# Two mixture-of-experts layers on one core: where the late steps' ends and rank products stand

## Chip, cores and metric

The kernel runs on one core of a Trainium2 chip. The metric is the device time of one execution in microseconds. The kernel before has a median of 907.2 us in three runs (906.87 to 910.54).

## What is computed

An attention over 4 batches, 8 heads and 576 positions gives 2304 rows of 512 numbers. Two mixture-of-experts layers follow, each with 8 experts of hidden width 1024, each row going to one expert:

```python
def _moe2_ref(x, w_gate, w1, w2) -> np.ndarray:
    N, D = x.shape
    E = w_gate.shape[1]
    logits = x @ w_gate
    expert_idx = np.argmax(logits, axis=1)
    ...
    for e in range(E):
        mask = expert_idx == e
        ...
        h = np.maximum(xe @ w1[e], 0.0)
        ye = h @ w2[e]
        out[mask] = gate_w[mask, None] * ye
    return out.astype(np.float32)
```

The first layer (layer 0) takes normalised rows and embeddings for its routing; its output is the second's (layer 1's) input. All arrays are float32.

## The kernel before

Rows are sorted by expert into tiles of 128. A layer is a row of **steps**, one tile and one expert each: 18 at least (`NT1`), up to 28 (`NS`), since each expert's last tile is partly filled. How many there are is known only on the chip. Steps 18 to 27 stand in nested conditions (`tc.If(nt_ > t)`; the jumps carry the lines of `nest.close()`, L1643 in layer 0, L1723 in layer 1); here steps 18 to 21 run and 22 to 27 are absent. Every engine that comes to step 22 jumps to the else branch of that condition, which waits for what the engine has issued and then raises its semaphores by as much as the absent steps would have raised them; so whatever waits for "the last write of this buffer" with an absent step as its last possible writer waits for that branch. POOL's else branch does so for its DMAs with one instruction, `INC_SWDGE_SEM`.

A step (`step`, L1374) has two products, each in three passes over high and low halves of the operands (`Wh` and `Wl`, the weights' halves; `b` and `x`, the activations'): 24 products of 512 columns into `ph0` and `ph1`, and 24 into `py`, in groups of three. ACT applies the Relu into `hs`, PE transposes it into `pt`, ACT and DVE split it into `b`. Where a step's expert is followed by another, its weights come by DMA into `stg`, and ACT (`split_hi`, L922) and DVE (`split_lo`, L925) split them into the buffer that is free.

`begin` (L1343) copies on POOL the four routing columns of the tile's gathered rows into `xca` and gathers the tile after next. `end` (L1350) scales `py` into `ysb` on ACT. In layer 0 POOL then copies the columns to `xcb` and stores `ysb` in `x2`, from which layer 1 gathers; in layer 1 POOL stores `ysb` in the output by an indirect DMA.

In layer 0 a step also routes the rows that the step before it made, for layer 1: PE transposes `ysb` and makes logits in `pm1` (columns 0 to 7), `route2` turns them on DVE and ACT into a one-hot `oh` and the gate weight in `xcb`; ACT's part is `th`, which reads `pm1`. `rank_pe` (L1334) makes two small products into columns 256 to 263 of the same `pm1`, `rank_ev` (L1338) and `place` evict and convert the ranks on DVE. Steps 2 to 16 rank in their middle the rows of two steps before; steps 16 and later (`late`) rank those of the step before, behind their last product. The columns in `xcb` go to `x2` by a DMA from POOL (L1474), for the last step by one from SP (L1681).

Program order within an engine is the order in which the code is written; each engine waits at the instruction that needs another's result. The program's own waits are by tile: `rank_pe` waits for `th`, though it writes other columns.

Of the kernel before, what the change touches and what calls it, by code (L numbers as in the profile page):

```python
# [409 lines left out]
def tile_kernel(ctx, tc, q, k, v, M_prev, z_prev, beta, emb, tau, w1a, w2a, wg, w1b, w2b, out):  # L410
    nc = tc.nc
    B, H, S, D = q.shape
    E, DM, FF = w1a.shape
    NTOK = B * S
    P = 128
    KD, KF = DM // P, FF // P
    NT1 = NTOK // P
    NE = 3
    NS = NT1 + E - 1 + NE
    XR = DM + 4  # L420
    PE_, ACT_, DVE_, SP_, POOL_ = (mybir.EngineType.PE, mybir.EngineType.Activation, mybir.EngineType.DVE, mybir.EngineType.SP, mybir.EngineType.Pool)
# [5 lines left out]
    x1, x2 = x1a[1:], x2a[1:]  # L427

    def ctile(shape, name, dt=F32):
        return cst.tile(shape, dt, name=name)  # L430
# [9 lines left out]
    xg0 = ctile([P, XR], "xg0")  # L440
# [7 lines left out]
    ctl, ini = ctile([P, 2, 8], "ctl", I32), ctile([P, 2, 8], "ini", I32)  # L448
# [133 lines left out]
    def place_(c0, n):  # L582

        sl = slice(c0, c0 + n)
        ri = rtile([P, 8], "ri", I32)[:, 0:n]
        r2 = rtile([P, 8], "r2", I32)[:, 0:n]
        rk = rtile([P, 8], "rk")[:, 0:n]
        V = nc.vector
        V.tensor_copy(ri, rkb[:, sl])
        yield  # L590
        V.tensor_scalar(out=r2, in0=ri, scalar1=7, scalar2=None, op0=ALU.arith_shift_right)
        yield
        V.tensor_scalar(out=ri, in0=ri, scalar1=127, scalar2=None, op0=ALU.bitwise_and)
        yield
        V.tensor_copy(tq[:, sl], r2)
        yield
        V.tensor_copy(rk, ri)
        yield
        V.tensor_tensor(out=ohp[:, sl], in0=iop.unsqueeze(1).to_broadcast([P, n, P]), in1=rk.unsqueeze(2).to_broadcast([P, n, P]), op=ALU.is_equal)

    def place(c0, n):
        for _ in place_(c0, n):
            pass

    class Route1:
# [32 lines left out]
        def rank_pe(self, ps):  # L638
            n, mm = self.n, nc.tensor.matmul
            self.ps = ps[:, 0:n * E].rearrange("p (n e) -> p n e", e=E)  # L640
            mm(ps[:, 0:n * E], tri, self.o.rearrange("p n e -> p (n e)"), start=True, stop=False)
            mm(self.ps, ones, acc.unsqueeze(1).to_broadcast([P, n, E]), start=False, stop=(n == 1))
            for i in range(n - 1):
                mm(self.ps[:, i + 1:], ones, self.o[:, i:i + 1].to_broadcast([P, n - 1 - i, E]), start=False, stop=(i == n - 2))
# [22 lines left out]
        def rank_ev(self):  # L667
            V = nc.vector
            V.tensor_tensor(out=self.t8, in0=self.o, in1=self.ps, op=ALU.mult)
            yield  # L670
            V.tensor_reduce(out=rkb[:, self.sl], in_=self.t8, axis=AX.X, op=ALU.add)
            yield
# [480 lines left out]
    def rows_of(t):  # L1153

        return xgt[t % 2] if t else xg0

    def gather(L, t):
        rows = src[L] if t >= NE else src[L][0:1 + P * (NT1 - (5, 2)[L])]
        return nc.gpsimd.indirect_dma_start(out=rows_of(t), out_offset=None, in_=rows, in_offset=bass.IndirectOffsetOnAxis(ap=idx[:, L, t:t + 1], axis=0))  # L1159
# [4 lines left out]

    xca = [ctile([P, 4], f"xca{i}") for i in range(2)]
    xcb = ctile([P, 4], "xcb")
    hooks = Hooks()
    tile_attention(tc, q, k, v, M_prev, z_prev, beta, ident, x1[:, 0:DM], xp, hooks)

# [131 lines left out]
    def yT_pe():  # L1301
        for kk in range(KD):
            nc.tensor.transpose(pm0[:, P * kk:P * kk + P], ysb[:, P * kk:P * kk + P], ident)

    def yT_ev(yT):
        nc.scalar.activation(out=yT, in_=pm0, func=AF.Copy)
# [31 lines left out]
    def rank_ev(c, count=True):  # L1338
        nc.vector.scalar_tensor_tensor(out=rs_["rj"], in0=pm1[:, 256:256 + E], scalar=1.0, in1=oh[:, c], op0=ALU.mult, op1=ALU.mult, accum_out=rkb[:, c:c + 1])
        if count:  # L1340
            nc.vector.tensor_tensor(out=acc, in0=acc, in1=oh[:, c], op=ALU.add)

    def begin(L, t):  # L1343

        if t:
            nc.gpsimd.tensor_copy(xca[t % 2], rows_of(t)[:, DM:XR])  # L1346
        if 1 < t < NS - 2:
            gather(L, t + 2)

    def end(L, t):  # L1350
        xc = xca[t % 2] if t else xg0[:, DM:XR]
        nc.scalar.activation(out=ysb, in_=py, func=AF.Copy, scale=xc[:, 0:1])  # L1352
        if L == 0:
            nc.gpsimd.tensor_copy(xcb, xc)
            nc.gpsimd.dma_start(out=x2[P * t:P * t + P, 0:DM], in_=ysb)
        else:
            nc.gpsimd.indirect_dma_start(out=out, out_offset=bass.IndirectOffsetOnAxis(ap=xc[:, 1:2].bitcast(I32), axis=0), in_=ysb, in_offset=None,  # L1357
                                         bounds_check=NTOK - 1, oob_is_err=False)

    def hT(i, b):  # L1360
        for kk in range(4):
            nc.tensor.transpose(pts[i][:, P * kk:P * kk + P], b.hs[i][:, P * kk:P * kk + P], ident)  # L1362
        hilo(pts[i], b.h[i])
# [10 lines left out]
    def step(L, t):  # L1374

        s, b = steps[L, t], bufs
        more = 0 < t < NS - 1
        split2 = t > 2
        rt2 = L == 0
        late = t >= NT1 - 2  # L1380
        x = x0 if t == 0 else b.x
        lx = lambda kk: (*x, P * kk)
        lh = lambda kk: (*b.h[kk // 4], P * (kk % 4))
        begin(L, t)
        s.gemm(0, ph0, lx, 0, 0, 3)
        yield
        s.gemm(0, ph0, lx, 0, 3, 9)
        yield
        s.gemm(0, ph0, lx, 0, 9, 12)
        if split2:  # L1390
            s.splits(0, (0, 1))
        nc.scalar.activation(out=b.hs[0], in_=ph0, func=AF.Relu)
        if split2:
            s.splits(1, (0,))

        ahead = (L, t) != (0, NT1 - 1)
        if ahead and split2:
            s.loads(0, (0, 1))
            s.loads(1, (0,))
        yield  # L1400
        s.gemm(0, ph1, lx, 512, 0, 6)
        hT(0, b)
        if rt2:
            yT_pe()
            yT_ev(b.hs[0])
        yield
        rk = L == 0 and 2 <= t <= NT1 - 2
        if rk:
            rank_pe(t - 2)
            rank_ev(t - 2)  # L1410
        s.gemm(0, ph1, lx, 512, 6, 12)
        last_mm[0] = s.lm[1]
        nc.scalar.activation(out=b.hs[1], in_=ph1, func=AF.Relu)
        yield
        if more:
            xT_pe(rows_of(t + 1))
        if rt2:
            parts_pe(b.hs[0])
            parts_ev(b.hs[0])
        if more:  # L1420
            hilo(psx, b.x)
        if rt2:
            route2_iov()
        s.gemm(1, py, lh, 0, 0, 3)
        if split2:
            s.splits(0, (2,), "h")
        hT(1, b)
        if split2:
            s.splits(0, (2,), "l")
        if more:  # L1430
            next_step(L, t + 1)
        yield
        s.gemm(1, py, lh, 0, 3, 6)
        cs = (1, 2, 3)
        if t == NE:
            s.splits(1, cs)
            cs = ()
        gen = iter(())
        if rt2:
            logits_pe(b.hs[0])  # L1440
        yield
        s.gemm(1, py, lh, 0, 6, 9)
        if rt2:
            gen = route2(t - 1)
        next(gen, None)
        next(gen, None)
        if split2:
            s.splits(0, (3,))
        if split2 and cs:
            s.splits(1, cs)  # L1450
        if t == 2:
            s.flags()
            s.splits(0, range(4))
            s.loads(0, range(4))
        if not ahead:
            e2.append(nc.values_load(ini[0:1, 1, 0:1], engines=[SP_], min_val=0, max_val=E - 1))
            s.loads(0, (0, 1))
            s.loads(1, (0,))
        if split2:
            s.loads(0, (2, 3))  # L1460
            s.loads(1, (1, 2, 3))
        drain(gen)
        if rk and ((t - 1) % 6 == 0 or t == NT1 - 2):
            c0 = (t - 2) // 6 * 6
            place(c0, t - 1 - c0)
        for q_ in range(9, 24, 3):
            yield
            s.gemm(1, py, lh, 0, q_, q_ + 3)
        last_mm[1] = s.lm[1]
        if (L, t) == (1, NT1 - 2):  # L1470

            nc.gpsimd.drain()
        if rt2:
            nc.gpsimd.dma_start(out=x2[P * (t - 1):P * t, DM:XR], in_=xcb)  # L1474
            if late:
                rank_pe(t - 1)
                rank_ev(t - 1)
                place(t - 1, 1)
        if not ahead:

            with tc.If(rg["nt"] <= NT1):
                for c in range(8):
                    for ins in split_chunk(c, rg["wv"]):
                        tc.add_to_no_dep_group("n18", ins)
        end(L, t)

    def abreast(a, b, ns=()):

# [104 lines left out]
    ysb = fp.tile([P, DM], F32, name="ysb")  # L1593
# [35 lines left out]
    for t in range(1, NS):  # L1629
# [11 lines left out]
        else:  # L1641
            drain(step(0, t))
    nest.close()  # L1643


    last_mm.clear()
# [65 lines left out]
    for t in range(1, NS):  # L1712
# [8 lines left out]
        else:  # L1721
            drain(step(1, t))
    nest.close()  # L1723


# [29 lines left out]
```

## Time and profile before

| | |
|---|---|
| median of 3 runs | 907.2 us |
| the profiled execution's own time | 905.06 us |
| its span, first to last instruction | 903.2 us |
| PE busy | 870.2 us, 96% |
| DVE, ACT, POOL busy | 502.1, 483.8, 275.3 us |
| mean granted clock of PE | 0.991 |

The span is what the trace shows; 1.86 us of the execution's own time lie around it. Times below are counted from the span's start. Layer 0's steps end at about 611 us, layer 1's at 895.8 us. A name like PEldq is the sequencer of PE, which handles jumps and waits ahead of the engine. `A <- B` in a wait reads: A waited for B.

### The profile page before, as it was taken

How to read it: one execution, taken by the hardware profiler on the slowest of the kernel's cores; microseconds unless marked ns; L12 is line 12 of the kernel's file. 1: busy time of each engine (PE TensorE's matmuls, PEld its weight loads, DVE VectorE, ACT ScalarE, POOL GpSimd, SP SyncE). 2: the span in 40 equal slices, each digit the busy share in tenths (PEclk: the TensorE clock that was granted, in tenths of full speed). 3: DMA queues.
4: the chain of work that ended last, by engine and by line, in shares of the span. 5: the costliest groups of instructions: out<-in, count | busy, mean ns of one | idle time of the engine just before them, and what ended most of it. 6: DMA issues, size and time to landing. Idle time of an engine off the chain costs nothing. (4 is left out here: it accounts for less than half of the span.)

```text
span 903.2 us, 20913 instructions
## 1 busy us (share of the span) xinstructions
PE 870.2 (96%) x5347; PEld 686.9 (76%) x5347; DVE 502.1 (56%) x1585; ACT 483.8 (54%) x972; POOL 275.3 (30%) x375
## 2 busy tenths in 40 slices
PE   6999999999989999998999999998999999999996
PEld 4777777677667777786888877886868888888885
DVE  4655656565684676379535666643567314463430
ACT  3657666666756735376435554532367435564531
POOL 5557635543633011212122312121231212321221
PEclk9999999999999999999999999998999999999998
DMA  7322352411333155359515317111668514384111
GB/s 130 80 52 82 73 170 78 101 40 41 100 111 113 59 211 175 108 165 314 177 49 164 108 37 235 38 49 40 234 203 297 171 48 139 130 305 135 43 38 39
DMA packets 102438, 110.32 MB, mean 122 GB/s; under 512 B 69882, under 2 KB 69882, under 8 KB 102276
## 3 DMA queue, kind: packets, MB, share of 16 engines
q1 hardware_dynamic: 94244, 85.33, 31.1%
q0 software_dynamic: 8032, 23.22, 7.8%
q8 instruction: 54, 0.88, 0.4%
q14 instruction: 108, 0.88, 0.3%
HBM read 90.32 MB, written 19.25 MB: 121 GB/s over the span
## 5 line engine op out<-in xcount | busy, mean ns | idle before, releaser
L1250 PE MATMUL py<-Wh,b 128*128 (+1 forms) x688 | 240.8, 406 | 2.6 <-DVE b L1194 2.4
L1250 PE MATMUL ph<-Wh,b 128*128 (+1 forms) x672 | 226.7, 398 | 0.5 <-ACTq L1261 0.5
L925 DVE TENSOR_TENSOR Wl<-stg,Wh 128x1024 f32 (+1 forms) x120 | 145.5, 1224 | 79.8 <-ACT Wh L922 74.4
L1250 PEld LDWEIGHTS py<-Wh,b 128*128 128x128 f32 x688 | 129.3, 188 | 32.6 <-issue 5.3
L1250 PEld LDWEIGHTS ph<-Wh,b 128*128 128x128 f32 x672 | 126.1, 188 | 26.7 <-ACTq L1261 0.9
L922 ACT ACTIVATE Wh<-stg 128x1024 f32 (+1 forms) x120 | 125.6, 1057 | 25.8 <-DVEq L1261 5.9
L1250 PE MATMUL py<-Wl,b 128*128 (+1 forms) x344 | 134.8, 392 | 0.0
L1250 PE MATMUL ph<-Wl,b 128*128 (+1 forms) x336 | 131.1, 390 | 2.7 <-DVEq L1261 2.7
L1194 DVE TENSOR_TENSOR b<-pt,b 128x512 fp32r<-128x512 f32 x86 | 59.4, 691 | 104.0 <-ACT b L1193 102.2
L287 ACT ACTIVATE att<-psat 128x512 f32<-128x512 f32 (+1 forms) x144 | 66.7, 463 | 70.6 <-PE psat L285 69.5
L308 PE MATMUL psav<-vb,att 128*128 128x128 f32 (+1 forms) x640 | 96.3, 281 | 2.9 <-ACT att L287 2.8
L308 PEld LDWEIGHTS psav<-vb,att 128*128 128x128 f32 x640 | 81.3, 191 | 17.3 <-ACT att L287 5.9
L1357 POOL DMA_INDIRECT out_dram<-ysb,xca x21 | 27.1, 1292 | 190.5 <-ACTq L1261 122.7
L1193 ACT ACTIVATE b<-pt 128x512 fp32r<-128x512 f32 x86 | 51.5, 598 | 62.9 <-PE pt L1362 61.4
L1250 PEld LDWEIGHTS ph<-Wl,b 128*128 128x128 f32 x336 | 63.2, 188 | 14.9 <-DVEq L1261 3.4
L1250 PEld LDWEIGHTS py<-Wl,b 128*128 128x128 f32 x344 | 64.9, 189 | 9.9
L233 DVE CUSTOM_DVE_ANT_0 a<-pss,wmask 128x128 f32<-128x128 f32 (+3 forms) x128 | 61.0, 485 | 19.2 <-PE pss L255 11.0
L268 ACT ACTIVATE a<-a,mx 128x128 f32<-128x128 f32 (+3 forms) x128 | 71.2, 556 | 0.4 <-DVE mx L233 0.3
L1352 ACT ACTIVATE ysb<-py,xca 128x512 f32<-128x512 f32 x42 | 28.8, 686 | 76.5 <-PE py L1250 65.8
L1159 POOL DMA_INDIRECT xg<-x_scratch,idx x48 | 55.6, 1157 | 38.4 <-issue 14.9
L1474 POOL DMA_DIRECT2D x_scratch<-xcb x21 | 11.9, 566 | 162.1 <-DVE xcb L1332 59.4
L285 PE MATMUL psat<-ident,a 128*128 128x128 f32 x320 | 56.9, 276 | 1.0 <-ACT a L268 0.8
(380 smaller groups left out, 1280.4 us busy)
## 6 DMA issues: line engine op xcount, KB each, us to landing
stg<-in_moe_w_dram SPq DMA_DIRECT2D x120, 512.0 KB
x_scratch<-ysb POOLq DMA_DIRECT2D x22, 256.0 KB
qkn<-in_q_dram SPq DMA_DIRECT2D x32, 128.0 KB
qkn<-in_k_dram SPq DMA_DIRECT2D x32, 128.0 KB
vb<-in_v_dram SPq DMA_DIRECT2D x32, 128.0 KB
x_scratch<-xb SPq DMA_DIRECT2D x16, 256.0 KB
x_scratch<-stg SPq DMA_DIRECT2D x11, 258.0 KB
xg<-x_scratch,idx POOLq DMA_INDIRECT x48
```

Source lines behind the costliest of these rows:

```text
L233: nc.vector.tensor_tensor_reduce(out=out, in0=ps, in1=mask, scale=1.0, scalar=bound, op0=ALU.add, op1=ALU.min, accum_out=m)
L268: nc.scalar.activation(out=a[:, 0:N], in_=a[:, 0:N], func=AF.Exp, scale=-1.0, bias=mx, accum_out=rs_t[pi][:, c, j:j + 1])
L285: nc.tensor.transpose(ps[:, 128 * i:128 * i + 128], x, ident)
L287: nc.scalar.activation(out=att[:, 0:N], in_=ps[:, 0:N], func=AF.Copy)
L308: nc.tensor.matmul(av_t[pi][:, c, j:], att[:, 128 * kb:128 * kb + 128], vn[:, kb, j:, 0:D], start=(kb == 0), stop=(kb == c))
L922: return nc.scalar.activation(out=chunk(Wh, c, wv), in_=stg[:, c].unsqueeze(1), func=AF.Copy).ins
L925: return nc.vector.tensor_tensor(out=chunk(Wl, c, wv), in0=stg[:, c].unsqueeze(1), in1=chunk(Wh, c, wv).bitcast(F32), op=ALU.subtract).ins
L1159: return nc.gpsimd.indirect_dma_start(out=rows_of(t), out_offset=None, in_=rows, in_offset=bass.IndirectOffsetOnAxis(ap=idx[:, L, t:t + 1] ...
L1193: nc.scalar.activation(out=hi, in_=ps, func=AF.Copy)
L1194: nc.vector.tensor_tensor(out=lo, in0=ps, in1=hi.bitcast(F32), op=ALU.subtract)
L1250: mm = nc.tensor.matmul(ps, x[:, col:col + P], W, start=(first and q_ == qs[0]), stop=(last and q_ == qs[-1]))
L1352: nc.scalar.activation(out=ysb, in_=py, func=AF.Copy, scale=xc[:, 0:1])
```

## The change

From step 17 on (`TE`), `end` of a step no longer stands at the step's end: it stands in `begin` of the next step, inside that step's condition, and for the last step that runs behind the whole nest, as `end(0, None)` and `end(1, None)`. The columns of steps 17 and later are copied into one buffer of their own, `xcn`, so that the end behind the nest need not know the step's number. Behind the nest of layer 0 SP, not POOL, stores `ysb`, at a row worked out from the number of steps, which it loads into a register. In steps 16 and later of layer 0 `rank_pe`, `rank_ev` and `place` stand ahead of the last two groups of three products, no longer behind the last.

```diff
--- before.py
+++ after.py
@@ -1164,6 +1164,7 @@
 
     xca = [ctile([P, 4], f"xca{i}") for i in range(2)]
     xcb = ctile([P, 4], "xcb")
+    xcn = ctile([P, 4], "xcn")
     hooks = Hooks()
     tile_attention(tc, q, k, v, M_prev, z_prev, beta, ident, x1[:, 0:DM], xp, hooks)
 
@@ -1340,19 +1341,32 @@
         if count:
             nc.vector.tensor_tensor(out=acc, in0=acc, in1=oh[:, c], op=ALU.add)
 
+
+    TE = NT1 - 1
+
+    def xc_of(t):
+        return xg0[:, DM:XR] if t == 0 else xca[t % 2] if t < TE else xcn
+
     def begin(L, t):
 
+        if t > TE:
+            end(L, t - 1)
         if t:
-            nc.gpsimd.tensor_copy(xca[t % 2], rows_of(t)[:, DM:XR])
+            nc.gpsimd.tensor_copy(xc_of(t), rows_of(t)[:, DM:XR])
         if 1 < t < NS - 2:
             gather(L, t + 2)
 
     def end(L, t):
-        xc = xca[t % 2] if t else xg0[:, DM:XR]
+
+        xc = xcn if t is None else xc_of(t)
         nc.scalar.activation(out=ysb, in_=py, func=AF.Copy, scale=xc[:, 0:1])
         if L == 0:
             nc.gpsimd.tensor_copy(xcb, xc)
-            nc.gpsimd.dma_start(out=x2[P * t:P * t + P, 0:DM], in_=ysb)
+            if t is None:
+                nl = nc.values_load(ini[0:1, 0, 3:4], engines=[SP_], min_val=NT1, max_val=NS)
+                nc.sync.dma_start(out=x2[bass.ds((nl - 1) * P, P), 0:DM], in_=ysb)
+            else:
+                nc.gpsimd.dma_start(out=x2[P * t:P * t + P, 0:DM], in_=ysb)
         else:
             nc.gpsimd.indirect_dma_start(out=out, out_offset=bass.IndirectOffsetOnAxis(ap=xc[:, 1:2].bitcast(I32), axis=0), in_=ysb, in_offset=None,
                                          bounds_check=NTOK - 1, oob_is_err=False)
@@ -1466,23 +1480,24 @@
         for q_ in range(9, 24, 3):
             yield
             s.gemm(1, py, lh, 0, q_, q_ + 3)
+            if late and rt2 and q_ == 15:
+                rank_pe(t - 1)
+                rank_ev(t - 1)
+                place(t - 1, 1)
         last_mm[1] = s.lm[1]
         if (L, t) == (1, NT1 - 2):
 
             nc.gpsimd.drain()
         if rt2:
             nc.gpsimd.dma_start(out=x2[P * (t - 1):P * t, DM:XR], in_=xcb)
-            if late:
-                rank_pe(t - 1)
-                rank_ev(t - 1)
-                place(t - 1, 1)
         if not ahead:
 
             with tc.If(rg["nt"] <= NT1):
                 for c in range(8):
                     for ins in split_chunk(c, rg["wv"]):
                         tc.add_to_no_dep_group("n18", ins)
-        end(L, t)
+        if t < TE:
+            end(L, t)
 
     def abreast(a, b, ns=()):
 
@@ -1641,6 +1656,7 @@
         else:
             drain(step(0, t))
     nest.close()
+    end(0, None)
 
 
     last_mm.clear()
@@ -1721,6 +1737,7 @@
         else:
             drain(step(1, t))
     nest.close()
+    end(1, None)
 
 
 # ---- launch: one core; inputs and outputs as the reference has them ----
```

Three places of the order. The first is PE at the end of a late step of layer 0 (this is step 19; the same piece stands in steps 16 to 27; `pm` is `pm1`, `Activation_49` and `DVE_49` are ACT's and DVE's semaphores). Before:

```order
L1250 MATMUL py<-Wh_4134,b_4237 128x512
L1250 REGISTER_ALU
L1250 MATMUL py<-Wl_4136,b_4237 128x512
L1250 MATMUL py<-Wh_4134,b_4238 128x512
L1335 LDWEIGHTS tri [waits DVE_49]
L1335 MATMUL pm_4141<-oh,tri 128x8 [waits Activation_49]
L1336 LDWEIGHTS ones
L1336 MATMUL pm_4141<-acc,ones 128x8
L1643 COMPARE_AND_BRANCH
L1250 ISA
L1250 MATMUL ph_4147<-Wh_4133,b_4233 128x512
```

Now:

```order
L1251 MATMUL py<-Wh_4135,b_4238 128x512
L1251 REGISTER_ALU
L1251 MATMUL py<-Wl_4137,b_4238 128x512
L1251 MATMUL py<-Wh_4135,b_4239 128x512
L1336 LDWEIGHTS tri [waits DVE_49]
L1336 MATMUL pm_4142<-oh,tri 128x8 [waits Activation_49]
L1337 LDWEIGHTS ones
L1337 MATMUL pm_4142<-acc,ones 128x8
L1251 ISA
L1251 MATMUL py<-Wh_4135,b_4238 128x512
L1251 REGISTER_ALU
L1251 MATMUL py<-Wl_4137,b_4238 128x512
```

The two rank products with their waits for `oh` (DVE) and `th` (ACT) stood behind the step's last product, and stand now with six products behind them.

The second is ACT at the end of layer 0: the last conditional step's `th`, the else branches (the row with x10) and layer 1's first instruction (L1306 or L1307). Before:

```order
L1277 UNCONDITIONAL_BRANCH
L1325 ACTIVATE th<-pm_4141,mn 128x8 [waits DVE_49]
L1352 ACTIVATE ysb<-py,xca_110 128x512 [waits DMASW1_49,PE_49,Pool_49]
L1643 UNCONDITIONAL_BRANCH
L1643 UNCONDITIONAL_BRANCH [waits Activation_49] x10
L1306 ACTIVATE hs_4229<-pm_4146 128x512 [waits PE_49,Activation_49]
```

Now:

```order
L1278 UNCONDITIONAL_BRANCH
L1326 ACTIVATE th<-pm_4142,mn 128x8 [waits DVE_49]
L1658 UNCONDITIONAL_BRANCH
L1658 UNCONDITIONAL_BRANCH [waits Activation_49] x10
L1362 ACTIVATE ysb<-py,xcn 128x512 [waits DMASW3_49,DMASW2_49,DMASW4_49,DMASW1_49,DMASW5_49,DMASW0_49,DMASW6_49,PE_49,DMASW7_49,Activation_49,Pool_49]
L1307 ACTIVATE hs_4230<-pm_4147 128x512 [waits PE_49,Activation_49]
```

`ysb` stood ahead of the jump and waits now behind it, for the counts of all eight POOL DMA semaphores (`DMASW`), which absent steps would have raised too.

The third is POOL at the end of layer 1, the last store of the output. Before:

```order
L1277 UNCONDITIONAL_BRANCH
L1357 DMA out_dram<-ysb,xca_110 2304x512 [waits DMASW5_49,Activation_49]
L1723 UNCONDITIONAL_BRANCH
L1723 ISA [waits Pool_49,DMASW6_49]
L1723 UNCONDITIONAL_BRANCH
```

Now:

```order
L1739 ISA [waits Pool_49,DMASW4_49,DMASW5_49,DMASW3_49,DMASW6_49,DMASW2_49,DMASW7_49,DMASW1_49,DMASW0_49]
L1739 UNCONDITIONAL_BRANCH
L1371 DMA out_dram<-ysb,xcn 2304x512 [waits DMASW4_49,DMASW5_49,DMASW3_49,DMASW7_49,DMASW1_49,Activation_49]
L1766 UNCONDITIONAL_BRANCH
L1766 ISA [waits barrier_Pool_Activation_PE_DVE_SP_gather]
```

The store stood ahead of the else branches (`ISA` is the instruction that raises the DMA semaphores) and stands now between them and the program's end (L1766).

## Rows read from the trace of the kernel before

**Rows 1.** Waits of PE from 285 us to the end: total us, times, longest
```profile
PE py L1250 <- DVE b L1194: 2.4, 2, 1.5
```

**Rows 2.** Line L1643, 609 to 619 us: ns min/median/max, first and last start
```profile
L1643 POOLq EVENT_SEMAPHORE  x5: 17/42/2449, 614.2 to 616.9; - x5
L1643 PEldq COMPARE_BRANCH  x2: 185/1751/3317, 609.3 to 612.8; - x2
L1643 ACTq COMPARE_BRANCH  x2: 38/42/45, 611.2 to 613.8; - x2
L1643 DVEq COMPARE_BRANCH  x2: 47/55/63, 612.2 to 615.4; - x2
L1643 POOLq COMPARE_BRANCH  x2: 38/42/45, 613.7 to 618.6; - x2
L1643 POOLq INC_SWDGE_SEM  x1: 1544/1544/1544, 617.0 to 617.0; - x1
```

**Rows 3.** Timeline at the end of layer 0: start, us, instruction, [idle before <-releaser]
```profile
608.76 0.27 ACT L1325 ACTIVATE th<-pm,mn 128x8 f32<-128x8 f32 x1 [2.00 <-DVE t8s L1320]
611.01 0.56 POOL L1474 DMA_DIRECT2D x_scratch<-xcb  x1 [9.62 <-DVE xcb L1332]
611.23 0.17 DVE L1339 SCALAR_TENSOR_TENSOR rj<-pm,oh 128x8 f32<-128x8 f32 x1 [0.52 <-PE pm L1336]
611.23 0.69 ACT L1352 ACTIVATE ysb<-py,xca 128x512 f32<-128x512 f32 x1 [2.21 <-PE pm L1336]
613.46 0.19 POOL L1354 COPY xcb<-xca 128x4 f32<-128x4 f32 x1 [1.89 <-DMA x_scratch<-xcb]
613.84 0.50 PE L1250 MATMUL ph<-Wh,x 128*128 x1 [2.65 <-ACTq L1643]
615.37 0.80 PE L1250 MATMUL ph<-Wl,x 128*128 x1 [1.04 <-DVEq L1643]
617.97 1.06 PE L1303 MATMUL pm<-ident,ysb 128*128 128x128 f32 x4
```

**Rows 4.** Two stretches: busy us of PE, PEld, DVE, ACT, POOL; granted clock; DMA
```profile
611.20:614.60 3.40, 0.50 (x1) 0.19 (x1) 1.15 (x9) 0.69 (x1) 1.10 (x3) 1.00 0.06 13
614.60:621.50 6.90, 6.13 (x15) 4.18 (x15) 0.23 (x1) 0.60 (x1) 1.13 (x2) 0.51 0.13 44
```

**Rows 5.** Timeline of layer 0's step 19
```profile
580.02 3.25 ACT L922 ACTIVATE Wh<-stg 128x1024 f32 x3 [0.78 <-DVEq L1261]
581.47 0.29 DVE L1323 TENSOR_SCALAR oh<-t8s,km,xcb 128x8 bf16<-128x8 f32 x1
581.88 0.62 PE L1250 MATMUL py<-Wh,b 128*128 x2
583.17 0.25 ACT L1325 ACTIVATE th<-pm,mn 128x8 f32<-128x8 f32 x1
583.47 0.18 PE L1335 MATMUL pm<-oh,tri 128*128 128x8 bf16 x1
```

**Rows 6.** Timeline of layer 0's step 18
```profile
567.99 0.29 DVE L1323 TENSOR_SCALAR oh<-t8s,km,xcb 128x8 bf16<-128x8 f32 x1
569.80 0.18 PE L1335 MATMUL pm<-oh,tri 128*128 128x8 bf16 x1
```

**Rows 7.** Timeline and line L1723 (as group 2) at the end of layer 1
```profile
896.90 1.02 POOL L1357 DMA_INDIRECT out_dram<-ysb,xca  x1 [9.79 <-ACT ysb L1352]
...
L1723 POOLq EVENT_SEMAPHORE  x5: 17/42/43, 900.5 to 900.8; - x5
```

**Rows 8.** Line L1749, the program's end, and DMA rate in 40 slices, 896 to 903.3 us
```profile
L1749 SPq EVENT_SEMAPHORE  x14: 17/28/28, 901.2 to 903.2; - x14
L1749 POOLq DRAIN  x3: 46/109/945, 901.5 to 903.0; - x3
L1749 SPq DRAIN  x3: 7/7/13, 902.0 to 902.7; - x3
...
GB/s 0 0 0 0 45 0 0 135 0 0 45 0 0 224 314 382 314 68 45 45 22 22 0 0 0 0 0 45 0 0 0 0 0 0 0 0 0 0 0 0
```

## Prediction

> **What bounds the kernel now.** PE is busy for 96% of the span, so I read the waits of PE first: from 285 us on there are few. The largest are two in a row at the end of layer 0, 2.65 and 1.04 us, for ACT's and DVE's sequencers [rows 3]; two stalls of 1.2 us on average on DVE's `b` come next [rows 1], in steps that the change does not touch. A step's end costs PE nothing in between: the next step's first product follows the last of `py` directly, and ACT scales `py` beside it. So moving the end inside running steps can gain nothing; only the places without a next step can: the end of layer 0, where layer 1 begins, and the end of layer 1, where nothing follows.
>
> **End of layer 0, now.** The jump over the absent steps is dear. ACT takes it at 611.2, with `ysb`, and has raised its semaphore at 613.8: 2.6 us. DVE takes it at 612.2, under the conversion of the ranks, and is through at 615.4: 3.1 us to its first wait behind it. PE's takes 3.32 us from 609.3, when its sequencer was ahead of the products [rows 2]. Layer 1's first product wants weights whose last possible writer is an absent step of ACT; it starts at 613.84, at ACT's semaphore. The second wants DVE's, and starts at 615.37, with 1.04 us idle [rows 3]. [...]
>
> **The change, part by part.**
>
> *Restart of layer 1: -0.48 us.* ACT's last work ahead of the jump is now `th`, dispatched at 608.76, so its semaphore comes near 608.8 + 2.6 = 611.4, before PE has ended its jump (609.3 + 3.32 = 612.6). ACT is out of it. DVE is not: the second product still waits for DVE's jump. The rank products come 6 x 0.227 = 1.36 us sooner, but `rj` at 611.23 had waited only 0.52 us for them [rows 3]; before that DVE was making `xcb`. So it starts at 610.75, its jump is taken 0.48 us sooner and the second product starts at 615.37 - 0.48 = 614.9. Bounds: a jump as short as ACT's 2.6 us gives -1.0; one as long as POOL's at the end (3.6 us, below) gives 0. I take its own 3.1.
>
> *The new stall in step 19: +1.36 us.* The rank products wait for `th` by the program's order. In step 19 ACT splits three weight chunks first (580.02, 3.25 us), and `th` runs from 583.17 to 583.42. The rank product ran at 583.47, behind the last product [rows 5]; its new place is six products, 583.24 - 581.88 = 1.36 us, earlier, at 582.11. PE gets there with `oh` ready (581.76) and `th` not, and takes instructions in order: it waits until 583.47 and the six products come behind. Nothing on PE later absorbs it [rows 1], so layer 0 ends 1.36 us later. This is the largest loss.
>
> *The other late steps: +0.15 us.* In step 18 `oh` ends at 568.28, and the rank's new place is 569.80 - 1.36 = 568.44 [rows 6]: 0.16 us of margin, less than the weight load of `tri` ahead of the product needs. In step 21 `th` is done at 609.03 [rows 3], some 0.6 us ahead of the rank's new place; steps 16, 17 and 20 have no splits ahead of it. 0 to 0.3 us together, an estimate of up to two such margins.
>
> *The last `ysb` of layer 0: nothing, if it is in time.* It waits now for POOL's else branch. POOL's jump follows the columns' store of 611.01, which has landed by 613.46, where the copy waiting for it starts [rows 3]; the branch waits for that landing (five waits 0.08 us apart, as in [rows 7]) and raises the DMA semaphores, which took 1.54 us [rows 2]: 615.4. ACT, as many waits and the scaling (0.69 us [rows 3]) later, has `ysb` at 616.4; PE wants it five products after the second, which was 2.60 us behind it [rows 3]: 614.9 + 2.6 = 617.5. Cover 1.1 us. SP's new store goes out while SP waits for the routing columns of the same rows, which DVE makes later in layer 1's first step; without that cover it would delay only POOL's later gathers.
>
> POOL's own jump here took 613.7 to 614.2, 0.5 us [rows 2], at the end of layer 1 up to 3.6 (below). [...] With 3.6 us the branch begins at 611.06 + 3.6 = 614.7, and `ysb` is there at about 617.7, 0.2 us late. The sum goes by 0.5.
>
> *End of layer 1: -1.4 us.* Now POOL issues the last store at 896.90 and jumps; its first wait in the else branch stands at 900.5, after which it raises the semaphores and, at 901.5, drains for 0.945 us; SP's last checks run from 901.2 to its own drain at 902.0, and the end is at 903.2 [rows 7, 8]. After the change POOL and ACT have jumped while PE still makes the last step's products (POOL's work in a step is over some 9.8 us before the store), so behind the store there is only the landing, SP's checks (0.8 us), and the barrier (0.8 us), POOL's drain lying beside them. The store's traffic thins from 899.1 and is over by 900.0 (slices of 0.18 us) [rows 8], POOL's wait puts the landing at 900.5 at the latest. End: landing + 1.7 us. With 899.6 it is 901.3 (-1.9), with 900.5 it is 902.2 (-1.0); I take the middle.
>
> *Inside the running steps: nothing.* `ysb` and POOL's copies and stores stand one branch later, about 0.04 us; ACT had 2.21 us idle before `ysb`, POOL 9.6 us before its store [rows 3]. Without that cover it would be 0.04 us in each of four steps.
>
> **Sum.** +1.36 + 0.15 - 0.48 - 1.4 = -0.37 us. On the profiled execution's own 905.06 us that is 904.7. The median of the runs shown lies 2.1 us above that execution; I add the sum to the median: 907.2 - 0.4 = **906.8 us**. By the bounds alone, 1.36 + 0 - 1.0 - 1.9 = -1.5 and 1.36 + 0.3 + 0 - 1.0 = +0.7: 905.7 to 907.9.
>
> **Rivals.**
>
> *The last `ysb` is late (slower).* Mechanism: POOL's jump and its raising of semaphores stand ahead of a transposition on PE that had no such wait. For it: the long waits of POOL [rows 2]. Against it: 1.1 us of cover at the low clock. It decides once `ysb` comes later than PE does, and that is easiest at the full clock, where the five products take about 1.3 us: PE arrives at 616.2, `ysb` in the worst case at 617.8, a wait of 1.6 us. With the small gain at the end: 907.2 + 1.36 + 0.15 - 0.48 + 1.6 - 1.0 = 908.8 us.
>
> *The clock does not fall (faster).* PE's idle time at the restart shrinks from 3.7 to about 3.2 us, in two pieces with a product between. Should the low stretch be missing, its 6.13 busy us [rows 4] would take half: -3.0, so 903.8 us. For it: PE stood still for up to 1.5 us elsewhere [rows 1] in a run whose mean clock is 0.991. Against it: 3.2 us is nearer to the 3.7 that came with the fall.
>
> *The stall of step 19 is not there.* If `th` came by 582.1, 905.4 us. Against it: the three splits stand ahead of it in ACT's order, and nothing of them is moved.
>
> *The end gains nothing.* If SP's checks and the landing cost what POOL's branch did (the jump was hidden behind the landing anyway), 908.2 us. For it: POOL's first wait and the landing lie within 0.5 us of each other.
>
> **How the numbers follow.** My case 0.55, `ysb` late 0.14, no fall of the clock 0.14, no stall in step 19 0.07, nothing at the end 0.10. The range takes in my own bounds and reaches to the first two rivals, with a little for the runs' own spread (3.7 us between three runs): 903.6 to 909.0. A difference of 0.5% is 4.5 us, about what a measurement of this kernel tells from none. No single case goes so far: faster takes the clock and the missing stall together (902.4), slower a late `ysb` with a longer low stretch of the clock. Faster 0.05, same 0.92, slower 0.03.
>
> **What would show it.** Right: in the waits of PE a new one of about 1.4 us of the rank product for `th` in step 19; the wait for ACT's jump gone, that for DVE's longer (1.2 us or more) with the second product about 3.7 us after the last of `py` instead of 4.2; the end 5.5 to 6.5 us after the last product instead of 7.4. Wrong: PE waiting for `ysb` at the transpositions of layer 1's first step; no wait for `th`; a granted clock of 1.00 all through layer 1's first step, or a low stretch much longer than 6.9 us.

## The result and the profile after

The changed kernel takes 915.96 us (median of 6 runs, 912.69 to 920.36); the kernel before, 907.42 (6 runs, 904.22 to 910.54). The ratio is 1.0109, 95% interval 1.0080 to 1.0139: slower by 8.5 us. I had forecast 906.8 and a range of 903.6 to 909.0. The profiled execution took 913.22 us, 8.2 more than the one of before; its page begins:

```profile
span 911.1 us, 20949 instructions
PE 878.5 (96%) x5347; PEld 687.7 (75%) x5347; DVE 500.3 (55%) x1585; ACT 484.1 (53%) x972; POOL 274.7 (30%) x374
```

PE is busy 8.3 us longer (870.2 before) with the same products, at a mean clock that is no lower (0.996 against 0.991). So most of the time is not in waits. The waits of PE in the changed kernel (total us, times, longest), the largest of the steps:

```profile
PE ph L1251 <- ACT ysb L1362: 5.2, 1, 5.2
PE ph L1251 <- DVEq L1262: 2.4, 2, 1.2
PE py L1251 <- DVE b L1195: 1.9, 2, 1.2
PE pm L1336 <- ACT th L1326: 1.1, 1, 1.1
```

The first stands for the two waits of [rows 3] at the restart, 3.7 us together. The last is the new stall of step 19.

**Where the time went.** I took the start of each step's two rows of products in both traces and looked at how the difference grows. It grows in nearly every step of both layers, by about 0.2 us a step, also where the change moves nothing. In the second half of one `py` (timeline of PE, a step of layer 1; the eight `Wl` products of a `py` are every third product, and these are the fifth and the last, 9 products apart), the kernel before:

```profile
757.57 0.39 PE L1250 MATMUL py<-Wl,b 128*128 x1
...
759.61 0.39 PE L1250 MATMUL py<-Wl,b 128*128 x1
```

and the changed kernel in the same step:

```profile
764.14 0.39 PE L1251 MATMUL py<-Wl,b 128*128 x1
...
766.24 0.40 PE L1251 MATMUL py<-Wl,b 128*128 x1
```

2.04 us against 2.10: a product is issued every 227 ns before, every 233 after, with no wait between and both at the granted clock 1.00. Over all products of layer 1's stretch from 640 to 890 us the median is 227 and 234 ns. Between the start of layer 0's first product and that of layer 1's last second product, 9.75 us are lost; some 6.5 of them are this pace, by the run with the tile alone below. Ahead of that stretch the changed kernel's trace is 0.9 us shorter (the one of before has a stretch at the low clock there, 283.5 to 286.9 us, which the other has not), and behind it the end gains 1.2.

The other places, as forecast or not. Step 19 (timeline): `th` has not moved in its step, PE waits 1.14 us for it, and the six products come behind; from the start of that step's second product to the next step's first, the change loses 1.35 us, as worked out (1.36). Some 0.1 of that is the pace; in the change without its tile, below, the same stretch loses 1.36 without it.

```profile
584.69 0.25 ACT L1326 ACTIVATE th<-pm,mn 128x8 f32<-128x8 f32 x1
584.99 0.17 PE L1336 MATMUL pm<-oh,tri 128*128 128x8 bf16 x1 [1.14 <-ACT th L1326]
```

The restart of layer 1. The jump's line, 609 to 621 us (columns as in [rows 2]):

```profile
L1658 ACTq COMPARE_BRANCH  x2: 38/42/45, 611.8 to 614.8; - x2
L1658 PEldq COMPARE_BRANCH  x2: 3071/3204/3338, 612.8 to 616.4; - x2
L1658 DVEq COMPARE_BRANCH  x2: 47/55/63, 615.0 to 618.1; - x2
```

The timeline of the same stretch:

```profile
614.02 0.40 PE L1251 MATMUL py<-Wh,b 128*128 x1
618.83 0.69 ACT L1362 ACTIVATE ysb<-py,xcn 128x512 f32<-128x512 f32 x1 [6.75 <-DMA x_scratch<-xcb]
619.60 0.79 PE L1251 MATMUL ph<-Wh,x 128*128 x1 [5.19 <-ACT ysb L1362]
622.32 0.93 PE L1304 MATMUL pm<-ident,ysb 128*128 128x128 f32 x4
```

Three stretches behind the last `py` product, as in [rows 4]:

```profile
614.40:619.50 5.10, 0.01 (x1) 0.00 (x0) 0.79 (x5) 0.67 (x1) 0.66 (x2) 1.00 0.04 10
619.50:622.30 2.80, 2.70 (x6) 2.04 (x7) 0.23 (x1) 0.02 (x1) 1.79 (x3) 0.51 0.46 120
622.30:626.00 3.70, 3.70 (x24) 2.74 (x23) 0.29 (x1) 1.20 (x2) 0.30 (x1) 0.91 0.47 132
```

Before, PE's second jump took 0.185 us [rows 2]; now it takes 3.07, from 616.4 to 619.4, and the first product starts right behind it. The row names `ysb` as what the product waited for; but in the program that product waits on ACT for the weights' split alone, which ACT's else branch had signalled at 614.7, and `ysb` happens to end at the same time. The changed kernel with 128 bytes, below, bears this out: there the first product starts 0.3 us before `ysb` ends, and the row of its wait names nothing:

```profile
PE ph L1253 <- issue: 5.0, 1, 5.0
```

In all five kernels whose layer 0 ends behind the nest (this one and four below) the product starts 0.16 us behind the end of PE's jump. `ysb` itself is ready 2.8 us ahead of its transposition.

The low clock lasts 3.4 us, not 6.9 [rows 4]: 0.51 up to 622.3, and 0.91 on the mean of the next 3.7 us, since it is back at 1.00 from 623.0. So the restart loses 2.7 us at its first product and has them back by its second row of products: 0.95 since the second product no longer waits (0.58 us behind the first, 1.53 before), the rest, 1.7 by an estimate, since 3.4 us fewer run at a granted clock of 0.51. The short stretch does not follow from the change alone. In the traces of the changed kernel with two tiles and with 128 bytes, which have the long jump too, the clock stays low for 6.8 us, and the restart costs 1.4 and 0.6 us; in the first of the runs with three distances, whose order is that of before, it is low for 3.4.

The end, in the timeline (before: [rows 7, 8]):

```profile
904.34 0.40 PE L1251 MATMUL py<-Wh,b 128*128 x1
905.73 0.69 ACT L1362 ACTIVATE ysb<-py,xcn 128x512 f32<-128x512 f32 x1 [5.21 <-PEq L1739]
906.69 1.01 POOL L1371 DMA_INDIRECT out_dram<-ysb,xcn  x1 [8.75 <-ACT ysb L1362]
```

and in the lines of layer 1's jump and of the program's end:

```profile
L1739 PEldq COMPARE_BRANCH  x2: 187/1799/3411, 902.0 to 905.7; - x2
L1766 SPq EVENT_SEMAPHORE  x13: 17/28/28, 909.4 to 911.0; - x13
```

From the start of the last product to the end it is 6.7 us, 7.9 before. The store comes 0.8 us later behind that product than before, since `ysb` waits for PE's jump (3.41 us): behind the nest, `py`'s last writer may be an absent step.

### The profile page after: what moved, and what is told of

It reads as the page before. It is cut to its first block, busy times and chain, and to the rows that moved or that the text cites. A ratio compares the mean times of both kernels' runs of the same rounds, so it can differ in the third digit from the quotient of the medians.

```text
span 911.1 us, 20949 instructions
## 1 busy us (share of the span) xinstructions
PE 878.5 (96%) x5347; PEld 687.7 (75%) x5347; DVE 500.3 (55%) x1585; ACT 484.1 (53%) x972; POOL 274.7 (30%) x374
## 5 line engine op out<-in xcount | busy, mean ns | idle before, releaser
L1251 PE MATMUL py<-Wh,b 128*128 (+1 forms) x688 | 244.1, 410 | 2.1 <-DVE b L1195 1.9
L1251 PE MATMUL ph<-Wh,b 128*128 (+1 forms) x672 | 230.2, 403 | 0.5 <-ACTq L1262 0.5
L1251 PE MATMUL ph<-Wl,b 128*128 (+1 forms) x336 | 133.5, 397 | 2.4 <-DVEq L1262 2.4
L1371 POOL DMA_INDIRECT out_dram<-ysb,xca x16 | 20.5, 1280 | 148.5 <-ACTq L1262 88.1
L1406 ACT ACTIVATE hs<-ph 128x512 f32<-128x512 f32 x42 | 25.0, 596 | 55.5 <-PE ph L1251 53.1
```

The source lines that it names most:

```text
L1251: mm = nc.tensor.matmul(ps, x[:, col:col + P], W, start=(first and q_ == qs[0]), stop=(last and q_ == qs[-1]))
```

## The experiments

Times are medians, or the time of one execution where it says so; the kernel before was run again beside each group. "Distance" is how far the tiles `b` stand behind the weights' tiles in a partition, modulo 256 bytes: 0 in the kernel before (`Wh0` at byte 69344, `b0` at 217056; the four weights' tiles, and the six `b`, agree modulo 256), 224 in the changed one, where the new tile `xcn` takes 32 bytes ahead of the weights.

**One tile, nothing moved.** Kernel before with

```diff
     xcb = ctile([P, 4], "xcb")
+    ctile([P, 4], "xcn")
```

> The kernel before, with one more tile of four columns behind xcb that nothing uses: the weights' tiles Wh and Wl stand 32 bytes higher in a partition, as in the changed kernel, and no instruction is moved. Placement theory: the 512-column products are issued every 234 ns in the median, not every 227, and the time is 7 to 9 us above before (914 to 916). Rival (the pace belongs to the moved instructions): 227 ns and 907. Rival (it is chance of the runs): no tie to the kernel, 905 to 910.

912.0 us against 905.49, ratio 1.0082 (1.0053 to 1.0111): 6.5 us. The pace is the changed kernel's, 9 products in 2.10 us:

```profile
759.67 0.40 PE L1251 MATMUL py<-Wl,b 128*128 x1
...
761.77 0.39 PE L1251 MATMUL py<-Wl,b 128*128 x1
```

A tile that no instruction touches costs three quarters of the loss. The instructions' order is excluded as the cause of the pace; the spread of the runs too.

**The changed kernel with a second unused tile** (distance 192).

> The changed kernel with a second unused tile, so that the weights' tiles stand 64 bytes higher than in the kernel before. If the place within 64 bytes decides: 227 ns between products, and about what I forecast plus the restart as traced, 907 to 908.5. If any shift costs: 234 ns and 916. If the moved instructions set the pace: 234 ns and 916.

909.84, ratio 1.0057 (1.0033 to 1.0082). Neither: the median is 230 ns in layer 1 and 231 in layer 0. 64 bytes further is better than 32 (234 in the changed kernel) and worse than none (227).

**Activations 32 bytes lower, weights in place** (distance 224), by a tile of four columns behind the `b` tiles.

> The kernel before, with an unused tile on the right side of the memory: the activations' tiles (x, hs, ysb, xg, b) stand 32 bytes lower, the weights where they were. If the weights' own place decides: 227 ns, 907. If the place of weights and activations relative to each other decides: 234 ns and 914 to 916.

913.46, ratio 1.0095 (1.0066 to 1.0124), 234 ns. It is not the weights' own place.

**Both** (distance 192).

> Both unused tiles: weights 32 bytes higher, activations 32 bytes lower, so that both have left their places within 64 bytes. If the weights' own place decides: 234 ns, 914 to 916. If the relative place decides: 227 ns, 907.

907.92, ratio 1.0032 (1.0013 to 1.0051), 229 ns in layer 1 and 231 in layer 0, which is neither of what I had expected. It is as in the second run, whose distance is the same: the distance decides, but not modulo 64.

**The changed kernel with 128 bytes** (xcn and three more tiles, distance 128).

> The changed kernel with three more unused tiles: the weights' tiles stand 128 bytes higher than in the kernel before, 96 higher than in the changed one. If the distance between weights and activations, taken modulo 128 bytes, sets the pace: 227 ns between products as in the kernel before, and what is left is the change's own: stall of step 19 +1.3, restart of layer 1 about 0 (a second jump of PE of 3 us against a shorter stretch at the low clock), end -1.2; 0 to +2 us against before, with the clock's low stretches as the difference. If only the old distance itself is good: 231 to 234 ns, +5 to +9 us.

914.91, ratio 1.0106 (1.0085 to 1.0126), 232 ns. The period is not 128 bytes. In two kernels further down which have the same distance (the end in layer 1 alone, and both ends) only the places of the moves can be read.

**The ranks alone, no tile.** `rank_pe`, `rank_ev` and `place` ahead of the last two groups, as in the diff.

> The kernel before, with only the ranks moved ahead of the last two groups; no tile is added. Stall theory: PE waits 1.1 us for th in step 19, layer 0 ends 1.3 us later; at the restart DVE's jump comes 0.5 us sooner but ACT's stays: +0.8 to +1.5 us. Rival (something later on PE absorbs the stall): 0.

907.43 against 905.47, ratio 1.0024 (1.0011 to 1.0036): +2.0 us. The late steps lose 1.33 us in the trace, and the stall is there:

```profile
585.36 0.25 ACT L1325 ACTIVATE th<-pm,mn 128x8 f32<-128x8 f32 x1
585.66 0.17 PE L1335 MATMUL pm<-oh,tri 128*128 128x8 bf16 x1 [1.20 <-ACT th L1325]
```

Behind the restart's second product PE stood still for another 1.56 us in this one profile; what held it the trace does not name.

**The end in layer 1 alone** (distance 128), `end` guarded with `L and`.

> The kernel before, with the end moved in layer 1 alone (the ranks and layer 0 stay; the tiles stand 128 bytes higher). With 227 ns between products: -1.2 us, the end 12.5 us after the last step's second product begins, not 13.7. With 231 to 234 ns the pace costs 4 to 9 us on top, and the end's 1.2 us is seen in the trace alone.

911.22, ratio 1.0079 (1.0057 to 1.0101): the pace's price. In the trace, last product to end: 6.92 us against 7.88.

**Both ends, ranks where they were** (distance 128).

> The changed kernel (tiles 128 bytes higher than before) with the ranks back behind the last product. Stall theory: no wait for th in step 19, 1.3 us less than the run with the ranks moved. At the restart DVE's jump comes as late as before, so the second product waits for it (about 4.2 us after the last of py) unless PE's second jump is the long one again (5.2 us).

910.9, ratio 1.0083 (1.0058 to 1.0109). No wait for `th`, and the late steps lose nothing but the pace. PE's second jump is the long one again, 2.95 us.

**The change without its tile.**

```diff
-    xcn = ctile([P, 4], "xcn")
+    xcn = xca[1]
```

> The change with all its moves, but without the new tile: xcn is the second of the two old buffers, xca1, which is free from step 17 on. Every tile stands where it stands in the kernel before. Placement theory: 227 ns between products; the steps drift by no more than 0.02 us each against before, and the time is before plus the moves: stall +1.3, restart -0.6 to +1.4, end -1.2, so -0.5 to +1.5 us; about 7 us less than the changed kernel. Rival (the moved instructions set the pace, and the tiles added theirs in the other runs): 234 ns and +8 us.

907.81 against 906.11, ratio 1.0014 (0.9996 to 1.0032): +1.7 us, where the change with the tile had +8.5. The pace is that of before:

```profile
758.75 0.39 PE L1251 MATMUL py<-Wl,b 128*128 x1
...
760.79 0.39 PE L1251 MATMUL py<-Wl,b 128*128 x1
```

This is the kernel that I had costed. Its trace against that of before: late steps of layer 0 +1.34 us, from there to layer 1's first second product -0.07, the rest of layer 1 +2.10, the end -0.72.

**The end in layer 1 alone, without a tile.**

> The kernel before with the end moved in layer 1 alone and xcn as xca1, no tile added. Placement theory: 227 ns between products, -1.2 us. Rival (the end's gain is inside the spread of the restart and cannot be timed): -0.3 to +0.3 us, with the 1.2 us in the trace.

904.11 against 906.11, ratio 0.9984 (0.9963 to 1.0005). The fastest by its median of the kernels that ran more than once; its interval still touches 1. Its trace shows 0.76 us of the 2.0 at the end: `ysb` waits for PE's jump here too,

```profile
896.33 0.69 ACT L1362 ACTIVATE ysb<-py,xca 128x512 f32<-128x512 f32 x1 [5.59 <-PEq L1738]
```

1.9 us behind the start of the last product, where before it came at 0.6.

**Kernel before, weights 256 bytes higher** (distance 0), and **32 bytes lower** (distance 32, `k1` and `ntl` put into one tile).

> The kernel before with an unused tile of 256 bytes a partition: the weights stand 256 bytes higher. If the distance to the activations counts modulo 256 bytes: 227 ns. If it does not: 229 to 234 ns.

> The kernel before with two small tiles put into one: the weights stand 32 bytes lower. If the pace depends on how far the distance is from the old one, to either side: 234 ns, as for 32 bytes higher. If one side is better than the other: below 227 or near 231 ns.

One execution each: 903.89 us and 227 ns; 911.81 us and 233 ns. 256 bytes more change nothing and 128 do, so the period is 256 bytes as far as these runs show; both sides of 0 are bad.

**Three distances in one program**, twice; the `b` tiles made 2304 bytes long and their content shifted inside:

```diff
-    ... fp.tile([P, 512], F32R, name=f"b{i}") if i < 6 ...
+    off = (4, 24, 40)
+    ... fp.tile([P, 576], F32R, name=f"b{i}")[:, off[i // 2]:off[i // 2] + 512] if i < 6 ...
```

> The kernel before, with the activations' tiles 2304 bytes long instead of 2048 and their content shifted inside: the two that the first product reads by 16 bytes, those of the first half of the second product by 96, those of its second half by 160; the weights stand as before. If a product's own two operands set its pace: three paces in one run, 230 to 236 ns for 96 and 160 (shifts of 32 to 128 gave 231 to 235), and for 16 a value between 227 and 235, or lower than 227 if the old place is not the best. If the pace belongs to the placement of the whole program: one pace in all three.

> As the run with 16, 96 and 160 bytes, with 4, 8 and 192 bytes. If own operands set the pace: 192 like 64 to the other side, about 231 ns; 4 and 8 near 227, or, if the pace falls off with the very first bytes, 230 to 235.

917.14 and 910.56 us beside 904.86, one execution each. The second run has `off = (1, 2, 48)`, which is 4, 8 and 192 bytes. In it the second half of `py` (192 bytes) is faster than the product of the next step that follows it (4 bytes). The first two rows of PE's timeline are six products apart, and so are the last two:

```profile
761.60 0.39 PE L1250 MATMUL py<-Wl,b 128*128 x1
...
762.97 0.39 PE L1250 MATMUL py<-Wl,b 128*128 x1
...
764.35 0.39 PE L1250 MATMUL ph<-Wl,b 128*128 x1
...
765.74 0.40 PE L1250 MATMUL ph<-Wl,b 128*128 x1
```

1.37 us (228 ns each) and 1.39 (232 ns). So the pace goes with the operands of the product itself, not with the program. Mean time from one product's start to the next, layer 1 from 640 to 890 us (pairs with a transposition between them left out; the first half of `py` takes some 231 also at distance 0, and stands apart: 231 at 8 bytes, 234 at 96):

| distance, bytes | ns | runs |
|---|---|---|
| 0 | 226.7 to 226.8 (`ph` 227.5 to 227.7) | before, ranks alone, change without tile, end of layer 1 without tile, 256 |
| 4 | 232.3 (`ph`) | second of the three-place runs |
| 16 | 233.3 (`ph`) | first of them |
| 32 | 233.2 | 32 bytes lower |
| 128 | 232.6 to 232.7 | three kernels with 128 bytes |
| 160 | 233.2 | first of the three-place runs |
| 192 | 228.7 to 228.9 | two tiles, both sides, second of the three-place runs |
| 224 | 233.3 to 233.4 | changed kernel, one tile, right side |

(Without `ph` the value is that of `py`'s second half.)

## Why the prediction was wrong

**The step that failed** is "Inside the running steps: nothing." It costed the two instructions that stand one branch later and not the tile that the same edit adds. `xcn` is allocated ahead of the weights' tiles, moves them by 32 bytes against the activations, and so slows most of the 2112 products: by 4 to 7 ns in `ph` and in the second half of `py`, by 0 to 2 in its first half. That is 6.5 us by the run with the tile alone. By the means it would be some 9, an estimate; a part comes back in waits (those for DVE's `b` shrink from 2.4 us [rows 1] to 1.9). No row of the trace of before shows it, since there all tiles stand at distance 0 (227 ns); what could have been seen ahead of the run is that the tile's line stands in front of the weights' allocation. The forecast, its range and all four rivals took the products' pace as given, so no case could hold the result.

**The moves**, read from the changed kernel and from the change without its tile:

- Stall of step 19, +1.36, and other late steps, +0.15: right. 1.34 together without the tile. Steps 16, 18 and 20 lose 0.32, 0.15 and 0.10 us in that trace and get nearly all of it back in the step behind. In step 18 I had held the load of `tri` to need more than the margin of 0.16 us; it takes 0.10 before and in the changed kernel, but from the end of `oh` to its start it is 0.19 there.
- Restart, -0.48: DVE's jump came as much earlier as worked out (its first wait behind it 4.0 us after the last `py` product began, 4.55 before), and ACT was out of it. But the bound was neither: PE's second jump took 3 us, and I had carried over its 0.185 us, so the second product came 5.8 us after the last of `py`, not 3.7. The jump was 2.8 to 3.1 us long in all five kernels with layer 0's end behind the nest and 0.18 to 0.19 in the eleven others. What makes it long or short no run shows. In the change without its tile the restart comes to -0.07 in sum, and that is in part luck: the low clock lasted 3.4 us in that trace too, and where it lasted 6.8 the same order lost 0.6 and 1.4.
- The last `ysb` of layer 0, nothing: right. It was there 5.5 us after the last `py` product began (5.65 worked out), and 2.8 us ahead of need, more than the cover of 1.1, since PE came late.
- End of layer 1, -1.4 (-1.0 to -1.9): too large. -1.16 in the changed kernel, -0.72 and -0.76 in the two without tile. I had let ACT's jump and POOL's count and forgotten PE's, for which `ysb` now waits: it is through 1.2 to 1.7 us after the last product begins.
- A low stretch of the clock that no case had: in a step of layer 1 PE waits 1.2 us for the split weights in the changed kernel; then the granted clock is 0.54 on the mean from 677.5 to 681.2, and the next row of products begins 1.6 us later. The kernel before waits as long in that step (1.23 us, to 674.1), and its clock stays at 1.00. Two stretches (columns as in [rows 4]):

```profile
677.50:681.20 3.70, 3.69 (x9) 2.92 (x10) 2.45 (x2) 2.11 (x2) 2.95 (x3) 0.54 0.88 309
681.20:684.00 2.80, 2.80 (x15) 2.29 (x15) 0.44 (x1) 1.78 (x3) 0.00 (x0) 1.00 1.01 364
```

It comes in seven of the sixteen profiles, with and without the change (in that of 256 bytes, which moves no instruction; not in that of the change with two tiles), so it is not shown to be a price of the change; it accounts for 1.58 of the 2.10 us in layer 1 of the change without its tile.

Without the tile the change measures +1.7 us (-0.4 to +2.9 by the interval) where my sum was -0.4. In its one trace the parts above come to +2.7: against my sum the end is 0.7 worse, the restart 0.4, the rest of layer 1 2.1 (the clock's 1.6 in it), the late steps 0.2 better.

The rivals: PE never waited for `ysb` at its transposition; the clock did fall; the stall of step 19 was there; the end gained about half.

## What to carry to other kernels

Where an edit adds, drops or resizes a tile, compare the addresses of the matmuls' operands before and after, and count what that does to their pace as a part of the edit (here 32 bytes took it from 227 to 234 ns): time the tile alone, or take a buffer that exists. A jump over absent work must be counted on every engine that a later instruction waits for, TensorE's too, and a jump's length is not carried over from another layout of the code (PE's second one took 0.185 us before and 3.07 in the changed kernel). What a trace names as released at the same moment is not always what was waited for: compare the wait in the program (here `ysb` ended at 619.52 and the product began at 619.60, but right behind PE's jump, which ended at 619.4).

## What the runs showed of the hardware

With float32r operands (the type of the halves) and 512 columns a product's issue interval depended in these runs on where its stationary tile (`b`, of which PE loads 128 columns) and its moving tile (the weights, 512 columns of them) stand to each other in a partition: 226.8 ns at equal place modulo 256 bytes, 228.8 at 192, 232.3 to 233.4 at 4, 16, 32, 128, 160 and 224. Some 6 ns in 227 hang on the two operands' places. At a granted clock of 0.51 no difference was seen: 427 ns in the kernel before and in the changed one. Why the distance counts no run shows; shown is the dependence on it, by three paces in one program. Whether a place exists that is faster than 227 ns was tried at nine other distances, and none was.
